# Seventy more products of the identity with itself, in front of two kinds of tile of a recurrence

## The chip, the cores and the metric

The kernel runs on 1 core of a Trainium2 chip. The metric is the device time of one execution in microseconds (us); the kernel before takes 1307.37 us, the median of 3 runs (1303.51 to 1311.31).

## The reference

The first stage is a recurrence. For each of 4 x 8 = 32 heads a state of 40 x 40 numbers is carried over 768 steps; inputs are r, k, v, w, a, b of shape (4, 8, 768, 40). Two products with weights follow on the 3072 x 320 result.

```
for t in range(768):
    y[t]  = r[t] @ state
    Sa    = state @ a[t]
    state = state * w[t][:, None] - outer(Sa, b[t]) + outer(v[t], k[t])
x = y, heads side by side                       # 3072 x 320
h = x @ moe_w_in;  x = (h * sigmoid(h)) @ moe_w_out      # 320 -> 2048 -> 320
out = (((x @ w1) * (x @ w2)) @ w3) @ w_out               # 320 -> 1024 -> 1024 -> 320
```

## The kernel before, in words

The recurrence is done in 12 chunks of 64 steps (`C`, `NCH`). Two heads share the 128 partitions, so there are 16 pairs, in 4 batches of 4. Inside a chunk the steps become small matrix products; only the state `Z` goes from chunk to chunk.

For two chunks at a time `prep` (L99) loads w, b, k, a and later r, clips w on DVE (L148), builds running products F and G on DVE (L106), multiplies the inputs by them, copies r into another layout on ACT (L207, `o<-in_`, from `in_r`), checks w with two ACTIVATE on ACT (L778, L779), and sends the results to DRAM; loads fetch them back in the layout of the products (`Rbd`, `Abd`, `Xt`, `Fn`). `A(c)` (L256) transposes (`px`, copied to `XT` by ACT at L267) and multiplies (`pl` L273). The 32 x 32 triangular blocks are inverted on POOL, and `merge` (L376) puts them together: TW is transposed on DVE (L380), `p` (L385, L397) are its products, ACT copies them (L387, L399).

`chain(c, b)` (L402) is the recurrence of one batch, in five steps with a `yield` between them; four chains are in flight. The steps are:

- `pp` (L414) and the old state `pss` (L423);
- `pu` (L435), copied into `UV` by DVE (L436) and ACT (L437). `UVb` is the `UV` of the fourth batch;
- `pz` (L443, L444), the products for the next state; DVE makes `Z` of it (L451, L452), and ACT copies `Z` into the next chunk's `UV` (L453, L454). Then `pv`, the transposes of `UV` (L457), copied to `VT` by ACT (L459). `VT` has two buffers;
- `pg` (L463), the products of `VT` with `Rbd`, masked into `GT` on DVE (L465);
- `py` (L472, L474), scaled into `x` on DVE (L477) and stored (`xd`) with SP.

`busy(p, n)` (L370; the rows call it L373) puts n products of the 128 x 128 identity with itself into a tile that the real products overwrite afterwards. It is called in front of `pu`, `pz` and the two `p` of `merge`. The numbers in front of it are: `MD` for `merge` (2 and 2 from chunk 2 on), `MC` = (0, 2) for `pu` and `pz`, and `MCC` = 2, the chunk from which `pu` and `pz` get none. So in the kernel before, chunks 0 and 1 have two such products before each `pz`, and no `pg` has any.

SP issues all DMAs, in order. Up to L1043 the order on the engines is that of the code; after it a list scheduler, run when the kernel is built, orders the instructions of every engine by its own estimate of when each can begin. An instruction that is added therefore moves others, on other engines too. From chunk 8 on, products for the weights (`w3ps` L581) and the first part of the second stage fill PE as well. After the recurrence `moe` (L658, L688) multiplies by the weights.

Of the kernel before, what the change touches and what calls it, by code (L numbers as in the profile page):

```python
# [24 lines left out]
class Kernel:  # L25
# [339 lines left out]
                s.nc.tensor.matmul(p, lhsT=s.idn, rhs=t[:, 0:512], start=True, stop=True)  # L365

    HC = 0
    MD, MC, MCC, ZT = (2, 2, 0), (0, 2), 2, 0

    def busy(s, p, n):  # L370

# [30 lines left out]
    def chain(s, c, b):  # L402
# [56 lines left out]
        ACT.copy(VT, pv[0:DP])  # L459
        yield 1280  # L460
        pg = s.PS([128, 4, 128], "pg")
        for hp in range(4):
            s.pe = nc.tensor.matmul(pg[:, hp], lhsT=VT[:, hp], rhs=Rbd[:, 4 * bb + hp], start=True, stop=True)  # L463
        GT = s.sm1.tile([128, 4, 128], F32, name="GT", bufs=2)
# [707 lines left out]
```

## Time and profile before

| | |
|---|---|
| median of 3 runs | 1307.37 us (1303.51 to 1311.31) |
| profiled execution | 1310.69 us, span 1309.0 us |
| PE busy | 1133.3 us (87%) |
| DVE, ACT, POOL busy | 695.7, 524.5, 309.8 us |
| granted TensorE clock, mean | 0.891 |

A row in time has its start, how long it ran, engine, line, operation, output and inputs, shapes and count; brackets hold the idle time of the engine just before and who ended it. PEclk is the granted clock of TensorE, as a share of 2.4 GHz: 0.50 is the lower of its two levels, 1.00 the upper. Lines are those of the kernel before; in the changed kernel lines after L368 stand one further down, lines after L461 two.

### The profile page before, as it was taken

How to read it: one execution, taken by the hardware profiler on the slowest of the kernel's cores; microseconds unless marked ns; L12 is line 12 of the kernel's file. 1: busy time of each engine (PE TensorE's matmuls, PEld its weight loads, DVE VectorE, ACT ScalarE, POOL GpSimd, SP SyncE). 2: the span in 40 equal slices, each digit the busy share in tenths (PEclk: the TensorE clock that was granted, in tenths of full speed). 3: DMA queues.
4: the chain of work that ended last, by engine and by line, in shares of the span. 5: the costliest groups of instructions: out<-in, count | busy, mean ns of one | idle time of the engine just before them, and what ended most of it. 6: DMA issues, size and time to landing. Idle time of an engine off the chain costs nothing. (4 is left out here: it accounts for less than half of the span.)

```text
span 1309.0 us, 25989 instructions
## 1 busy us (share of the span) xinstructions
PE 1133.3 (87%) x10416; PEld 995.9 (76%) x10416; DVE 695.7 (53%) x1358; ACT 524.5 (40%) x1156; POOL 309.8 (24%) x540
## 2 busy tenths in 40 slices
PE   2874768985978899997886999999999999999996
PEld 1654657885867888886675888889889889978985
DVE  7685772456487676758998531234424423433431
ACT  4555433353455454355455432233323323322321
POOL 4142600270551836503555102100000000000000
PEclk9885775687786899998988999999999999999998
DMA  9958787277388743667412000110001001000000
GB/s 211 192 101 180 135 145 145 48 137 159 69 175 196 146 106 75 192 175 217 121 31 61 1 1 1 36 27 20 1 1 41 1 1 36 6 1 21 1 1 23
DMA packets 258273, 105.86 MB, mean 81 GB/s; under 512 B 226400, under 2 KB 246880, under 8 KB 258144
## 3 DMA queue, kind: packets, MB, share of 16 engines
q1 hardware_dynamic: 258144, 104.12, 36.1%
q8 instruction: 84, 1.38, 0.5%
q14 instruction: 45, 0.37, 0.1%
HBM read 75.24 MB, written 28.84 MB: 80 GB/s over the span
## 5 line engine op out<-in xcount | busy, mean ns | idle before, releaser
L658 PE MATMUL hp<-xH,w 128*128 128x512 f32 x704 | 249.6, 397 | 2.7 <-ACT xH L487 2.7
L688 PE MATMUL yp<-w,gH 128*128 128x320 f32 x1152 | 234.0, 315 | 13.7 <-ACT gH L487 13.6
L666 DVE TENSOR_TENSOR sg<-sg,hp 128x512 f32<-128x512 f32 x144 | 99.0, 687 | 230.8 <-ACT sg L665 150.3
L688 PEld LDWEIGHTS yp<-w,gH 128*128 128x128 f32 x1152 | 193.1, 192 | 27.8 <-ACT gH L487 17.5
L487 ACT CAST gH<-sg 128x512 fp32r<-128x512 f32 x144 | 89.3, 620 | 161.7 <-DVE sg L666 106.1
L658 PEld LDWEIGHTS hp<-xH,w 128*128 128x128 f32 x704 | 131.8, 188 | 28.9 <-ACT xH L487 3.7
L488 DVE TENSOR_TENSOR gL<-sg,gH 128x512 fp32r<-128x512 f32 x120 | 83.0, 692 | 130.6 <-ACT gH L487 89.4
L688 PE MATMUL yp<-w,gL 128*128 128x320 f32 x576 | 147.5, 312 | 0.3 <-POOL gL L488 0.3
L658 PE MATMUL hp<-xL,w 128*128 128x512 f32 x352 | 139.2, 395 | 0.0
L688 PEld LDWEIGHTS yp<-w,gL 128*128 128x128 f32 x576 | 102.0, 190 | 2.4 <-POOL gL L488 0.7
L342 POOL TENSOR_TENSOR tmp<-T,L 128x87 f32<-128x87 f32 (+31 forms) x186 | 93.2, 501 | 42.3 <-DVE L L325 28.2
L665 ACT ACTIVATE sg<-hp 128x512 f32<-128x512 f32 x96 | 57.3, 597 | 109.3 <-PE hp L658 93.1
L346 POOL TENSOR_TENSOR T<-T,tmp 128x87 f32<-128x87 f32 (+31 forms) x186 | 96.8, 520 | 14.4
L273 PE MATMUL pl<-Abd,XT 104*128 104x128 f32 x384 | 66.4, 332 | 24.0 <-ACT XT L267 13.4
L273 PEld LDWEIGHTS pl<-Abd,XT 104*128 104x128 f32 x384 | 59.6, 238 | 26.9 <-ACT XT L267 12.8
L658 PEld LDWEIGHTS hp<-xL,w 128*128 128x128 f32 x352 | 66.4, 189 | 11.6
L463 PE MATMUL pg<-Rbd,VT 104*128 104x128 f32 x384 | 56.8, 309 | 21.2 <-ACT VT L459 15.5
L463 PEld LDWEIGHTS pg<-Rbd,VT 104*128 104x128 f32 x384 | 53.4, 220 | 23.0 <-ACT VT L459 16.8
L658 PE MATMUL hp<-xA,w 128*128 128x512 f32 x176 | 69.4, 395 | 0.0
L665 ACT COPY sg<-hp 128x512 f32<-128x512 f32 x48 | 28.2, 587 | 101.8 <-PE hp L658 64.5
L658 PE MATMUL hp<-xB,w 128*128 128x512 f32 x176 | 68.0, 394 | 0.0
L737 POOL COPY row<-row 128x64 f32<-128x64 f32 x24 | 5.5, 249 | 250.0 <-DVE row L700 142.8
(249 smaller groups left out, 2079.0 us busy)
## 6 DMA issues: line engine op xcount, KB each, us to landing
w3q<-in_moe_w_dram SPq DMA_DIRECT2D x16, 512.0 KB
wq<-in_moe_w_out_dram SPq DMA_DIRECT2D x24, 320.0 KB
wq<-in_moe_w_in_dram SPq DMA_DIRECT2D x16, 256.0 KB
wq<-in_moe_w_dram SPq DMA_DIRECT2D x16, 256.0 KB
Xt<-Bd SPq DMA_DIRECT2D x24, 160.0 KB
Xt<-Kd SPq DMA_DIRECT2D x24, 160.0 KB
Abd<-Ad SPq DMA_DIRECT2D x48, 80.0 KB
Fd<-F SPq DMA_DIRECT2D x12, 320.0 KB
```

Source lines behind the costliest of these rows:

```text
L273: nc.tensor.matmul(pl[:, hp], lhsT=XT[b][:, hp], rhs=Abd[b // 2][0:DP, 4 * (b % 2) + hp], start=True, stop=True)
L342: e.tensor_tensor(out=t3, in0=T[:, a:b, j : j + 1].to_broadcast([128, n, m]), in1=L[:, j : j + 1, j + 1 : 32].to_broadcast([128, n, m]), o ...
L346: s.last = e.tensor_tensor(out=T[:, a:b, j + 1 : 32], in0=T[:, a:b, j + 1 : 32], in1=t3, op=ALU.add)
L463: s.pe = nc.tensor.matmul(pg[:, hp], lhsT=VT[:, hp], rhs=Rbd[:, 4 * bb + hp], start=True, stop=True)
L487: s.nc.scalar.copy(hi, raw)
L488: (eng or s.nc.vector).tensor_tensor(out=lo, in0=raw, in1=hi, op=ALU.subtract)
L658: nc.tensor.matmul(p, lhsT=a, rhs=b, start=j == 0, stop=j == 7)
L665: nc.scalar.activation(out=sg, in_=p, func=func) if func else nc.scalar.copy(sg, p)
L666: nc.vector.tensor_tensor(out=sg, in0=sg, in1=q, op=ALU.mult)
L688: nc.tensor.matmul(y, lhsT=a[:, sl], rhs=W[:, b], start=first and j == 0, stop=last and j == 2)
L737: nc.gpsimd.tensor_copy(r[:, 320:384], r[:, 256:320])
```

## The change

`MCC` goes from 2 to 7, so the two products before `pz` are there for chunks 2 to 6 as well, in all four batches: 5 x 4 x 2 = 40. A new `MG` = (1, 6, 3) puts three products before `pg` in chunks 2 to 6 for batches 0 and 1: 5 x 2 x 3 = 30. Nothing that the kernel outputs depends on them.

```diff
-    MD, MC, MCC, ZT = (2, 2, 0), (0, 2), 2, 0
+    MD, MC, MCC, ZT = (2, 2, 0), (0, 2), 7, 0
+    MG = (1, 6, 3)
 ...
         pg = s.PS([128, 4, 128], "pg")
+        s.busy(pg, s.MG[2] if b < 2 and s.MG[0] < c <= s.MG[1] else 0)
         for hp in range(4):
```

The list scheduler also moves other instructions. The first place is ACT in chunk 5, from the second `VT` to the checks of `prep`; `UV` and `UVb` from `Z` are the next state's copies, `F` and `G` the first copies of `prep`. Before:

```order
L459 COPY VT<-pv 104x512
L150 COPY F<-in__3849 128x4x40
L151 COPY G<-in__3849 128x4x40
L453 COPY UV_595<-Z 40x4x40
L454 COPY UV_595<-Z 40x4x40
L453 COPY UV_595<-Z 40x4x40
L454 COPY UV_595<-Z 40x4x40
L459 COPY VT<-pv 104x512
L453 COPY UVb_597<-Z 40x4x40
L454 COPY UVb_597<-Z 40x4x40
L459 COPY VT<-pv 104x512
L778 ACTIVATE in__3849<-in__3849,small 128x1280
```

And in the changed kernel:

```order
L460 COPY VT<-pv 104x512
L454 COPY UV_595<-Z 40x4x40
L455 COPY UV_595<-Z 40x4x40
L454 COPY UV_595<-Z 40x4x40
L455 COPY UV_595<-Z 40x4x40
L454 COPY UVb_597<-Z 40x4x40
L455 COPY UVb_597<-Z 40x4x40
L780 ACTIVATE in__3891<-in__3891,small 128x1280
L460 COPY VT<-pv 104x512
L163 COPY G<-F 64x40
L781 ACTIVATE in__3891,small<-in__3891,small 128x1280
L460 COPY VT<-pv 104x512
```

The third `VT` stood behind six of the state's copies in chunk 5 and in front of the last two; now it stands behind all eight and behind the first check, and the fourth behind the second check.

The second place is ACT in chunk 6, around the copy of r (`o`), up to the first `UV` copy of the chunk. Before:

```order
L418 COPY Pb_233<-pp 64x4x40 x2
L429 COPY Sst_243<-pss 40x160 x2
L207 COPY o<-in__4495 128x1280
L267 COPY XT<-px 104x512
L418 COPY Pb_235<-pp 64x4x40 x2
L487 CAST wo_4693<-wr 128x320 x2
L429 COPY Sst_245<-pss 40x160 x2
L267 COPY XT<-px 104x512
L387 COPY TW<-p_4359 32x512 x2
L437 COPY UV_595<-pu 64x4x40
```

And in the changed kernel:

```order
L430 COPY Sst_243<-pss 40x160 x2
L267 COPY XT<-px 104x512
L489 CAST wo_4763<-wr 128x320 x2
L419 COPY Pb_235<-pp 64x4x40 x2
L430 COPY Sst_245<-pss 40x160 x2
L267 COPY XT<-px 104x512
L388 COPY TW<-p_4415 32x512 x2
L489 CAST wo_4874<-wr 128x320 x2
L207 COPY o<-in__4551 128x1280
L438 COPY UV_595<-pu 64x4x40
```

The copy of r stood in front of the third `XT`, and now stands behind `XT` and `TW`, just in front of the copy of the first `UV`.

The third place is SP at the end of chunk 5: the four loads of r for chunk 6 (`in_` from `in_r`), the stores of x (`xd`) and of the products (`Bd`, `Kd`, `Ad`), and the loads of `Fn`. Before:

```order
L51 DMA Fn<-Fd_81 64x8x40 x2
L51 DMA in__4495<-in_r_dram 32x1280
L51 DMA Fd_83<-F 64x1280 x2
L51 DMA in__4495<-in_r_dram 32x1280 x2
L51 DMA Rbd_227<-Rd_93 40x8x64 x2
L51 DMA w3q<-in_moe_w_dram 128x1024
L51 DMA in__4495<-in_r_dram 32x1280
L51 DMA wq_4240<-in_moe_w_out_dram 128x640
L51 DMA Bd_77<-in__3865 64x1280 x2
L51 DMA wq_4240<-in_moe_w_out_dram 128x640
L51 DMA Kd_71<-in__4128 64x1280 x2
L51 DMA xd_1_107<-x 256x1x40 x4
```

And in the changed kernel:

```order
L51 DMA Kd_71<-in__4184 64x1280 x2
L51 DMA Fn<-Fd_81 64x8x40 x2
L51 DMA Rbd_227<-Rd_93 40x8x64
L51 DMA xd_1_107<-x 256x1x40 x4
L51 DMA Rbd_227<-Rd_93 40x8x64
L51 DMA w3q<-in_moe_w_dram 128x1024 x2
L51 DMA Ad_89<-o 2560x1x32 x2
L51 DMA Fn<-Fd_81 64x8x40 x2
L51 DMA in__4551<-in_r_dram 32x1280 x4
L51 DMA wq_4296<-in_moe_w_out_dram 128x640 x2
```

The loads of r stood in front of the stores of `Bd`, `Kd` and the second `xd`; now they stand behind these, two `w3q`, `Ad` and two `Fn`.

## Rows read from the trace of the kernel before

**Rows 1.** Stretches of the span. Columns: the window and its length, busy time of each engine (instructions), PEclk, DMA share, GB/s.

```profile
180.00:640.00 460.00, 395.54 (x6044) 356.80 (x6044) 292.96 (x578) 216.84 (x543) 177.42 (x294) 0.82 0.62 140
193.50:241.00 47.50, 43.10 (x593) 38.76 (x593) 12.97 (x17) 16.75 (x38) 0.00 (x0) 0.50 0.62 119
251.50:265.00 13.50, 13.35 (x178) 12.69 (x180) 3.51 (x7) 3.03 (x10) 11.56 (x26) 0.50 0.22 46
337.00:343.50 6.50, 5.80 (x60) 4.69 (x60) 5.05 (x13) 5.36 (x15) 2.53 (x7) 0.50 0.23 50
374.50:381.00 6.50, 4.80 (x21) 4.71 (x22) 6.30 (x15) 2.46 (x6) 4.60 (x12) 0.50 1.10 199
388.00:398.00 10.00, 10.00 (x162) 9.18 (x161) 9.93 (x24) 4.30 (x13) 0.00 (x0) 0.50 0.60 142
421.00:425.50 4.50, 4.50 (x48) 3.43 (x48) 4.47 (x11) 3.47 (x11) 1.77 (x3) 0.51 0.89 137
```

**Rows 2.** PE in time, chunk 1. Start, duration, instruction, in brackets the idle time before it and its releaser.

```profile
184.40 0.61 PE L373 MATMUL pz<-idn 128*128 128x128 f32 x4
184.94 0.25 PE L443 MATMUL pz<-UV,Xt 128*64 128x40 f32 x1
...
193.30 4.03 PE L463 MATMUL pg<-Rbd,VT 104*128 104x128 f32 x16 [3.73 <-ACT VT L459]
```

**Rows 3.** PE in time: a product pg of chunks 2, 3, 5 and 6.

```profile
251.65 3.78 PE L463 MATMUL pg<-Rbd,VT 104*128 104x128 f32 x16 [2.16 <-ACT VT L459]
...
286.08 3.98 PE L463 MATMUL pg<-Rbd,VT 104*128 104x128 f32 x16 [3.95 <-ACT VT L459]
...
376.19 3.95 PE L463 MATMUL pg<-Rbd,VT 104*128 104x128 f32 x16 [4.40 <-ACT VT L459]
...
430.12 2.05 PE L463 MATMUL pg<-Rbd,VT 104*128 104x128 f32 x16 [0.60 <-ACT VT L459]
```

**Rows 4.** PE in time: before and in chunk 4, then before and in chunk 6.

```profile
308.91 1.92 PE L385 MATMUL p<-TW,L 32*32 32x32 f32 x64 [8.74 <-DVE TW L380]
...
340.18 0.29 PE L444 MATMUL pz<-UV,Xt 128*40 128x40 f32 x1 [0.70 <-ACT UV L437]
...
410.81 2.08 PE L273 MATMUL pl<-Abd,XT 104*128 104x128 f32 x8 [4.31 <-ACT XT L267]
...
421.21 0.33 PE L443 MATMUL pz<-UV,Xt 128*64 128x40 f32 x1
```

**Rows 5.** ACT in time, chunk 5: the third and fourth VT and a check.

```profile
375.56 0.58 ACT L459 COPY VT<-pv 104x512 f32<-104x512 f32 x1
377.43 0.58 ACT L459 COPY VT<-pv 104x512 f32<-104x512 f32 x1
382.30 1.36 ACT L778 ACTIVATE in__3849<-in__3849,small 128x1280 f32<-128x1280 f32 x1 [4.29 <-DVE G L106]
```

**Rows 6.** ACT and DVE in time: the r of chunk 6, and x of chunk 5.

```profile
407.48 2.67 ACT L207 COPY o<-in__4495 128x1280 f32<-128x1280 f32 x1 [6.96 <-DMA in__4495<-in_r_dram]
...
402.28 0.48 DVE L477 TENSOR_TENSOR x<-py,Fn 128x320 f32<-128x320 f32 x1
```

**Rows 7.** SP in time, chunks 5 to 6. Start, time at the queue's head, instruction.

```profile
394.13 1.29 SPq L51 DMA_DIRECT2D Fn<-Fd  x2
395.53 0.57 SPq L51 DMA_DIRECT2D in__4495<-in_r_dram  x1
...
401.73 0.82 SPq L51 DMA_DIRECT2D in__4495<-in_r_dram  x1
...
407.83 3.79 SPq L51 DMA_DIRECT2D xd<-x  x4
...
412.32 4.00 SPq L51 DMA_DIRECT2D Ad<-o  x2
416.37 3.20 SPq L51 DMA_DIRECT2D Fn<-Fd  x2
```

**Rows 8.** PE in time: a wait in chunk 8.

```profile
499.24 0.23 PE L444 MATMUL pz<-UV,Xt 128*40 128x40 f32 x1 [1.87 <-ACT UV L437]
```


## Prediction

> **What bounds the kernel now.** I first read the stretches of the span [rows 1]. Between 180 and 640 us, where the changed chunks lie, PE is busy for 395.5 of 460 us, but at a mean granted clock of 0.82: the clock goes between its two levels. It is at the lower one, 1.2 GHz, for example in 193.5-241, 251.5-265, 374.5-381 and 388-398. So PE is the bound there in two ways, by its work and by a clock that halves it, and the reader is to see that PE is busy in nearly the whole of some slow stretches (13.35 of 13.5 us).
>
> Then I read PE in time, with the idle time in front of each row. In chunks 2, 3 and 5 a `pg` waits for its `VT` copy, for 2.16, 3.95 and 4.40 us, and in chunk 6 for 0.60 [rows 3]; in each of the first three the clock is at the lower level right behind the wait. Other waits have nothing to do with `pg`: 8.74 us for `TW` at 308.91, which DVE makes late since the data of `prep` come late, and 4.31 us for `XT` at 410.81 [rows 4]. For that one I read ACT: `XT` stands behind the copy of r, which waits 6.96 us for its load [rows 6]. So in these chunks loads and the order on ACT and SP set the pace as often as PE's work.
>
> **The change, part by part.**
>
> *The products themselves.* Two products (a product leaves two records) begin at 184.40 and the next instruction at 184.94 [rows 2], at the upper clock: 0.27 us each, and I take twice that, 0.54, at the lower. Seventy cost 18.9 us of PE at the upper clock. In each of the chunks 2 to 6 it is 8 x 0.27 = 2.16 before `pz` and 6 x 0.27 = 1.62 before `pg`, 3.78 in all. What covers them are the waits that follow them on PE:
> - Chunks 3 and 5: waits of 3.95 and 4.40 [rows 3] hold the 3.78. Nothing is paid.
> - Chunk 2: 2.16 holds part, 1.6 is left over; but before chunk 4 PE has 8.74 us of idle time for `TW` [rows 4], set by loads. If that cover were gone, 1.6 us would be paid.
> - Chunk 4: its `pg` do not wait; a `pz` waits 0.70 [rows 4]. 3.78 - 0.70 = 3.1 are on PE's path. What comes next is chunk 6's first `pz`, which, below, is set by SP and ACT and not by PE, and so I count these 3.1 at nothing; the cover is the 4.31 us of idle time at 410.81. If it is gone they are paid in full.
> - Chunk 6: 3.78 - 0.60 = 3.2 at most [rows 3]. The first pair before `pz`, 0.54, lies in a wait (below), and the 1.62 before `pg` beside the wait for `VT`, whose copies ACT then does late. That leaves 2.16 - 0.54 = **+1.6**.
>
> *The third and fourth `VT` of chunk 5.* ACT did them at 375.56 and 377.43, and the first check at 382.30 [rows 5]. In the new order the third stands behind the last two state copies, which ended by 377.43, and behind the check of 1.36 us: 377.43 + 1.36 = 378.8, at least 3.2 us later. If the check runs no earlier than before, it is 382.30 + 1.36 = 383.7, 8.1 us later. The check waits for the products of `prep` on DVE, and the fewer masks stand among these, the earlier it can run; I take +3.6, near the lower end. Of this wait nothing is queued behind on PE but `pg`, `py` and the store of x; the price is paid through SP.
>
> *The copy of r of chunk 6.* This is the largest term. Before, its four loads left SP between 395.53 and 402.55, and the copy ran 4.9 us after that, at 407.48, for 2.67 us [rows 6, 7]. Now the loads stand behind the second `xd`, `Ad` and two `Fn`, and the first `UV` copy of chunk 6, which the first `pz` needs, stands behind the copy. SP is busy without a pause there, so taking the loads out lets it come earlier by what they then take again, and the last load leaves when the `Fn` did, at 416.37 + 3.20 = 419.57 [rows 7]. Then 4.9 to land, 2.67 to copy and about 0.3 for the `UV` copy give 427.5, against the first `pz` at 421.21 [rows 4]: +6.3. From below: the pair of `Fn` took only 1.29 at 394.13 [rows 7], so 1.9 of its 3.20 may be a wait that goes: +4.4. From above: the second `xd` needs x, written at 402.76 [rows 6]. With the third `VT` 3.6 later that is 406.4. Without the loads, which took at least 4 x 0.57 = 2.3, SP would come to it at 405.5; so SP waits 0.9: +7.2. With `VT` 5.7 later it would wait 3.0: +9.3. I take the middle of 4.4 and 7.2, **+5.8**. What goes in exchange, the wait of `XT` at 410.81, is worth nothing then, since `UV` is late next.
>
> *Chunk 8.* The scheduler moves twelve weight products into the 1.87 us in which a `pz` waits for `UV` [rows 8]. They have to be done anyway: **-1.9**.
>
> *The clock.* I take 0. A chunk that already has these products shows why: chunk 1 has two before each `pz`, and yet its `pg` waited 3.73 for `VT` at 193.30 and the clock was at 1.2 GHz from 193.5 to 241, though PE was busy for 43.1 of these 47.5 us [rows 1, 2]. The bounds are a gain of 14.8 (the first rival) and, where the clock falls in one more stretch like 388-398, a loss of half its 10.0 us, 5.0.
>
> The Trainium skill has a rule here, in "TensorE: Matmul & The Clock Gate", section "Part 4: PE-mode transpose": transposes do not count as activity for the clock in the way that products do. By it plain products put between transposes would be worth more than their busy time tells, which is the first rival. What the trace shows of it is mixed: the last 4.5 us before the clock rose at 425.5 held `pz` products and transposes in turn, with PE busy all the time [rows 1]; no row has transposes alone.
>
> The sum: 5.8 + 1.6 - 1.9 = +5.5. The profiled execution took 1310.7, so 1316.2 in its terms; it lies 3.3 above the median of the runs, which makes **1312.9**.
>
> **The rivals.**
>
> *A: the clock stays up (faster).* The added 3.78 us nearly fill the waits that the slow stretches follow. For it: in chunk 2 the wait of 2.16 is less than what is put in front of it, and in chunk 5 4.40 would be 0.6. If the clock rose in chunks 4 to 6, half of PE's busy time in the slow stretches would come back [rows 1]: 2.9 (337-343.5), 2.4 (374.5-381), 5.0 (388-398), 2.2 (421-425.5), 12.5 in all. With 3.1 + 3.2 paid for products and chunk 8's -1.9 this is -8.1, so 1299.3; with chunk 2's 13.35 / 2 = 6.7 carried through too, -14.8, 1292.6. I take the middle, **1296**. Against it: chunk 1, and that in chunk 5 the wait grows by what `VT` is later. Early gains must also pass 8.74 us of waiting for loads.
>
> *B: everything that I covered is paid (slower).* The place is SP. Chunk 4's 3.1 delay its x and with it the loads of `prep` queued behind; the third `VT` is 5.7 later, midway between its bounds; the copy of r then holds the first `pz` of chunk 6 by 9.3, and chunk 6 pays 3.2. 3.1 + 9.3 + 3.2 - 1.9 = +13.7, **1321**. It decides if the third `VT` of chunk 5 runs later than 380. For it: SP has hardly a pause in the rows, so what is late there stays late. Against: each of the three terms would have to come near its upper bound.
>
> *C: the products are hidden, and the order changes cancel.* Then it is 1307, inside the forecast's own range.
>
> **How the numbers follow.** The forecast, with C, has a chance of 0.45 and its own range is 1307 to 1317: below its middle if r's loads come early, above if the clock costs something. A has 0.27 (1292 to 1301), B 0.28 (1314 to 1325). This kernel can't be told from no change within 0.5%, 6.5 us: 1300.8 to 1313.9. Faster: 0.25 of A and 0.02 of the forecast, 0.27. Same: 0.33 of the forecast, 0.02 of A, 0.01 of B, 0.36. Slower: 0.10 of the forecast and 0.27 of B, 0.37. The range of 1295 to 1322 leaves out a third of A's chance and a third of B's, some 0.19.
>
> **What would show it.** Products at 0.27 and 0.54 us each. In chunks 2, 3 and 5: whether `pg`'s wait for `VT` shrinks by about 3.8, and whether the clock stays at 1.00 behind it; if it does in chunks 4 to 6, A is right. In chunk 5: the third `VT` against the last state copy. In chunk 6: the copy of r just in front of the first `UV` copy, its loads leaving SP behind `Fn`, and the first `pz` some 6 us later against the same chunk before; if the copy of r ends before PE is done with `pu`, my largest term is wrong and the result is near 1307 or below. In chunk 8: no wait of 1.87. From 640 on nothing should differ but a shift.

## The result and the profile after

The changed kernel took 1324.97 us (median of 4 runs, 1321.43 to 1326.06) against 1306.13 for the kernel before beside it (4 runs, 1303.51 to 1311.31): ratio 1.0141, 95% interval 1.0111 to 1.0170, or 18.8 us slower. The forecast of 1312.9 is wrong and so is its range, which ended at 1322. The profiled execution took 1324.17 us, 13.5 more than the one of before.

The products are there. Lines of the source in the changed kernel, between 180 and 450 us: operation, count, then the shortest, the median and the longest record in ns. A product leaves two records, and 8 of the 88 belong to chunk 1.

```profile
L374 PE MATMUL pz<-idn x88: 273/275/421, 180.5 to 431.5; 128*128 128x128 f32 x88
L374 PE MATMUL pg<-idn x60: 273/275/275, 239.7 to 435.4; 128*128 128x128 f32 x60
```

The clock did rise. To compare the same work in kernels that run at different times, I use the second addition `x` (`x<-py`, DVE) of a chunk as a mark. From chunk 1's mark to the last `x`, the kernel before and then the changed kernel; the third row is a stretch of the changed kernel in chunk 6:

```profile
211.28:628.56 417.28, 359.43 (x5620) 324.06 (x5617) 260.76 (x516) 200.47 (x506) 170.16 (x288) 0.83 0.62 139
206.80:639.31 432.51, 363.24 (x5760) 330.01 (x5757) 259.85 (x517) 200.43 (x506) 178.72 (x288) 0.87 0.60 134
416.00:432.00 16.00, 8.89 (x74) 7.74 (x75) 13.08 (x26) 11.15 (x22) 5.11 (x9) 0.50 0.80 156
```

The mean granted clock is 0.87 where it was 0.83. PE has 140 records more, the 70 products, and its busy time grew by 3.8 us only, from 359.4 to 363.2, though the products alone are 18.9 at the upper clock. The stretch grew by 15.2. So three quarters of what grew, 11.4 us, is time in which PE waits. The third row is one place, chunk 6, where PE is busy for 8.9 of 16 us.

PE in time, changed kernel: a `pg` of chunk 3, a `pg` and a `p` of chunk 5, and a `pz` of chunk 6.

```profile
280.28 4.28 PE L465 MATMUL pg<-Rbd,VT 104*128 104x128 f32 x16 [7.17 <-ACT VT L460]
...
372.24 4.27 PE L465 MATMUL pg<-Rbd,VT 104*128 104x128 f32 x16 [4.79 <-ACT VT L460]
...
383.62 1.92 PE L386 MATMUL p<-TW,L 32*32 32x32 f32 x64 [3.45 <-DVE TW L381]
...
419.67 0.29 PE L445 MATMUL pz<-UV,Xt 128*40 128x40 f32 x1 [7.50 <-ACT UV L438]
```

The wait of `pg` in chunk 5 did not shrink from 4.40 by the products [rows 3], it is 4.79. Chunk 3's grew from 3.95 to 7.17. The 7.50 before `pz` in chunk 6 answers to no wait at all [rows 4]. ACT in the same kernel, chunk 5 and then chunk 6:

```profile
370.35 1.36 ACT L780 ACTIVATE in__3891<-in__3891,small 128x1280 f32<-128x1280 f32 x1
371.62 0.56 ACT L460 COPY VT<-pv 104x512 f32<-104x512 f32 x1
...
416.63 2.67 ACT L207 COPY o<-in__4551 128x1280 f32<-128x1280 f32 x1 [9.42 <-DMA in__4551<-in_r_dram]
419.33 0.29 ACT L438 COPY UV<-pu 64x160 f32<-64x160 f32 x1
```

The check of 1.36 us stands right in front of the third `VT`, and the copy of r, 2.67 us, right in front of the first `UV`. Both are as the order said. The time of r's loads on SP, at the queue's head:

```profile
389.35 3.91 SPq L51 DMA_DIRECT2D xd<-x  x4
...
407.38 3.54 SPq L51 DMA_DIRECT2D Fn<-Fd  x2
410.97 2.99 SPq L51 DMA_DIRECT2D in__4551<-in_r_dram  x4
```

The last load of r leaves at 413.96 and the copy starts 2.7 us later; before, SP's last left at 402.55 and the copy ran at 407.48 [rows 6, 7].

To place the loss in time I go by the marks, in one execution each. *Chunks 2 to 4* runs from chunk 1's mark to chunk 4's, *5 and 6* from there to chunk 6's, *7 on* to the last `x`, *behind* to the end of the span. The kernels below the second row are the experiments.

| us in the profiled execution | chunks 2 to 4 | 5 and 6 | 7 on | behind |
|---|---|---|---|---|
| before | 144.2 | 80.9 | 192.1 | 680.4 |
| after | 140.9 | 95.0 | 196.6 | 683.1 |
| products_old_order | 142.7 | 82.7 | 195.2 | 680.9 |
| new_order_no_products | 146.9 | 92.6 | 193.2 | 681.7 |
| new_order_in_chunk_5 | 140.2 | 89.6 | 195.0 | 681.3 |
| new_order_in_chunk_6 | 138.7 | 88.0 | 193.7 | 681.5 |
| new_order_in_5_6 | 138.1 | 95.2 | 192.9 | 680.9 |
| new_order_to_chunk_4 | 147.2 | 82.3 | 194.3 | 681.5 |
| new_order_but_5_6 | 146.8 | 84.3 | 196.6 | 681.1 |
| loads_early | 141.8 | 86.4 | 195.1 | 683.2 |

Chunks 5 and 6 took 14.1 us longer than before. The 3.3 gained ahead of them are within what executions differ by: the kernels with before's order and the products took from 138.1 to 142.7 there. The new order gains nothing in chunks 2 to 4 and may lose there. In eight traces with the products and the new order up to chunk 4 (further kernels below among them), chunk 4's mark comes at 347.7 to 355.5 us, 351.8 in the mean; in the seven with the products and before's order there, at 343.5 to 352.3, 347.8 in the mean.

### The profile page after: what moved, and what is told of

Read it like the earlier page. It is cut to its first block, busy times and chain, and to the rows that moved or that the text cites. A ratio compares the mean times of both kernels' runs of the same rounds, so it can differ in the third digit from the quotient of the medians.

```text
span 1322.4 us, 26273 instructions
## 1 busy us (share of the span) xinstructions
PE 1135.7 (86%) x10556; PEld 999.1 (76%) x10556; DVE 695.9 (53%) x1358; ACT 524.8 (40%) x1156; POOL 318.5 (24%) x540
## 5 line engine op out<-in xcount | busy, mean ns | idle before, releaser
L690 PE MATMUL yp<-w,gH 128*128 128x320 f32 x1152 | 232.2, 314 | 12.4 <-ACT gH L489 12.3
L342 POOL TENSOR_TENSOR tmp<-T,L 128x87 f32<-128x87 f32 (+31 forms) x186 | 98.5, 530 | 40.5 <-DVE L L325 26.2
L346 POOL TENSOR_TENSOR T<-T,tmp 128x87 f32<-128x87 f32 (+31 forms) x186 | 100.4, 540 | 14.3
L273 PE MATMUL pl<-Abd,XT 104*128 104x128 f32 x384 | 59.3, 307 | 23.0 <-ACT XT L267 12.0
L465 PE MATMUL pg<-Rbd,VT 104*128 104x128 f32 x384 | 55.8, 301 | 24.8 <-ACT VT L460 18.8
L273 PEld LDWEIGHTS pl<-Abd,XT 104*128 104x128 f32 x384 | 53.4, 216 | 25.3 <-ACT XT L267 13.1
```

The costliest lines, as they stand in the source:

```text
L273: nc.tensor.matmul(pl[:, hp], lhsT=XT[b][:, hp], rhs=Abd[b // 2][0:DP, 4 * (b % 2) + hp], start=True, stop=True)
L342: e.tensor_tensor(out=t3, in0=T[:, a:b, j : j + 1].to_broadcast([128, n, m]), in1=L[:, j : j + 1, j + 1 : 32].to_broadcast([128, n, m]), o ...
L346: s.last = e.tensor_tensor(out=T[:, a:b, j + 1 : 32], in0=T[:, a:b, j + 1 : 32], in1=t3, op=ALU.add)
L690: nc.tensor.matmul(y, lhsT=a[:, sl], rhs=W[:, b], start=first and j == 0, stop=last and j == 2)
```

## The experiments

All times are ratios to runs of before on the same chip, with 95% intervals; us are these times 1307.

**Products or order?** A table lists each engine's instructions in a wanted order, and each is made to follow the one before it by an order-only dependency (`NoSync`):

```diff
+    def fix(s, packed, extra):
...
+                        s.tc.add_manual_dep(k, last.name, info, reason="fix")
...
+            s.fix(ORDER, s.added)
```

No run holds the kernel before to its own order and changes nothing else, so what this itself may cost is in the figures that follow.

*products_old_order* has the 70 products and before's order:

> All 70 products of the change, but every instruction on every engine in the order of the kernel before, by order-only dependencies; a product stands just in front of the pz or pg that it belongs to. Theory O (the moved order is the loss, above all the copy of r in front of the first UV copy of chunk 6; the products with the clock are a gain): 1295 to 1302, with the waits of pg in chunks 2, 3 and 5 shorter and more of 180 to 420 us at the upper clock. Rival P (the products' own time on PE is the loss): 70 x 0.27 = 18.9 more than before, about 1325. Rival C (products hidden and clock gains lost to loads): 1306, within 3.

Measured: 1.0037 (1.0010 to 1.0065), median 1310.71. *new_order_no_products* has the changed kernel's order and none of the products:

> None of the 70 products, but every instruction on every engine in the order of the changed kernel. Theory O: slower than the changed kernel or equal, 1322 to 1335, with the copy of r of chunk 6 again just in front of the first UV copy and PE waiting about 7 us there. Rival P: 1306, as before. Rival C: 1325, as the changed kernel.

Measured: 1.0143 (1.0094 to 1.0192), median 1326.58, the whole loss without the work that was added. In before's order the products cost some 4.8 us (1.3 to 8.5) of their 18.9; the order costs the rest, some 13.6. In the new order they cost nothing more that these runs can tell. The clock shows what the products give back. From chunk 1's mark to chunk 4's, before and then products_old_order:

```profile
211.28:355.53 144.25, 117.96 (x1717) 105.84 (x1714) 67.40 (x129) 63.09 (x148) 47.47 (x91) 0.71 0.57 105
```

```profile
205.90:348.55 142.65, 121.79 (x1801) 110.95 (x1797) 68.16 (x128) 63.27 (x148) 49.80 (x92) 0.78 0.55 106
```

The granted clock there is 0.78 with the products and 0.71 without. In new_order_no_products it is 0.74 and in the changed kernel 0.83. Over all kernels here it is 0.71 to 0.76 in the three that lack the products in these chunks, and 0.76 to 0.83 in the others.

*chunks_2_to_4* keeps the products in chunks 2 to 4 alone and lets the scheduler order anew:

```diff
-    MD, MC, MCC, ZT = (2, 2, 0), (0, 2), 7, 0
-    MG = (1, 6, 3)
+    MD, MC, MCC, ZT = (2, 2, 0), (0, 2), 5, 0
+    MG = (1, 4, 3)
```

> The products only in chunks 2 to 4 (24 before pz, 18 before pg), the order left to the scheduler, which puts the copy of r of chunk 6 behind most of that chunk's UV copies. Theory O: the early gain of the changed kernel (7 us at chunk 5) without the loss of chunk 6: 1296 to 1303. Rival P: 42 x 0.27 = 11.3 more than before, 1317.

Measured: 1.0090 (1.0063 to 1.0118). Slower too, in a third order. Its profiled execution was the shortest of ten, 1309.06 against a median of 1318.92, and so doesn't say where.

**Is it the copy of r in chunk 6?** *r_after_uv* holds that copy behind the `UV` copies:

```diff
-        ACT.copy(o, r.rearrange("p t e -> p e t"))
+        with s.tc.issue_after(s.uv.ins) if g == 5 else ExitStack():
+            ACT.copy(o, r.rearrange("p t e -> p e t"))
```

The scheduler then moves some other instructions too, further on in the program.

> The changed kernel, with the copy of r of chunk 6 put behind the copies of UV of that chunk on ACT (one order-only dependency; the scheduler then moves a few other instructions). Its load leaves SP as late as in the changed kernel. Theory O: the wait of 7.50 us of the first pz of chunk 6 goes and the time falls by 8 to 14, to 1311 to 1317. Rival P and a rival in which that wait only hides another one: within 3 of 1325.

Measured: 1.0142 (1.0088 to 1.0196), nothing won. PE still waits in front of `pz`, for DVE's copy `A` now (DVE's row below):

```profile
421.50 1.22 PE L375 MATMUL pz<-idn 128*128 128x128 f32 x4 [7.65 <-DVE A L275]
```

```profile
419.99 0.33 DVE L499 TENSOR_SCALAR wr<-wq 128x320 int32<-128x320 int32 x1 [11.42 <-DMA wq<-in_moe_w_out_dram]
```

In the new order a weight tile `wr` that waits 11.42 us for its load stands in front of the copies that PE needs. The next three take it, and then the loads:

*weights_moved* (DVE, chunk 6; its cast `wo` on ACT goes along):

```diff
 TENSOR_TENSOR A<-pl,msk
-TENSOR_SCALAR wr<-wq
-SCALAR_TENSOR_TENSOR wr<-wq,wr
-TENSOR_TENSOR A<-pl,msk
-TENSOR_SCALAR wr<-wq
...
+TENSOR_SCALAR wr<-wq
+SCALAR_TENSOR_TENSOR wr<-wq,wr
 TENSOR_TENSOR Z<-pz,Z
```

> As the run before, but only the weight tile's conversion is moved; the copy of r stays in front of the first UV copy of chunk 6. Theory D: the copy of r still holds the first pz, 1321 to 1327. Rival E (the weight tile alone was the cause, and the copy of r is beside it): 1312 to 1317.

*r_and_weights_moved* has both edits:

> The changed kernel with its products, every instruction in the order of the changed kernel by order-only dependencies, but two things moved behind the last UV copy (UVb) of chunk 6: the copy of r on ACT, and on DVE the conversion of one weight tile (six wr<-wq, with the first of the two casts on ACT and the subtraction on POOL that follow it). Theory D (two waits lie side by side in chunk 6: ACT waits for the load of r, DVE for the load of a weight tile that SP issues just behind it, and either alone holds the first pz): the wait of 7.5 us goes, chunk 6 is reached 8 to 11 us earlier, 1312 to 1317. Rival S (the loss is spread over many moved instructions): within 4 of 1325.

*loads_early* has neither, and puts the four loads of r on SP behind the first `Fn`, in front of the second `xd`, and two loads of the weight tile in front of `Ad`:

```diff
 DMA Fn<-Fd
+DMA in_<-in_r_dram x4
 DMA Rbd<-Rd
...
+DMA wq<-in_moe_w_out_dram x2
 DMA Ad<-o
 DMA Fn<-Fd
-DMA in_<-in_r_dram x4
-DMA wq<-in_moe_w_out_dram x2
```

> The changed kernel with its products and its order, but on SP alone the four loads of r of chunk 6 stand in front of the second xd of chunk 5 (behind the first two Fn), and the two loads of the weight tile in front of Ad. ACT and DVE keep their order. Theory D: both waits shrink by most of their 7 to 10 us and the time falls by 6 to 10, 1315 to 1319, since the place on ACT and DVE only costs because SP brings the data late. Rival S: within 4 of 1325.

Measured: 1.0138 (1.0104 to 1.0171), 1.0123 (1.0099 to 1.0148) and 1.0119 (1.0088 to 1.0150). None brings back more than 3 us in the median. With both moved the wait before `pz` did go, and two others came, for a `VT` that now stands behind the copy of r. PE, r_and_weights_moved:

```profile
417.83 0.23 PE L450 MATMUL pz<-UV,Xt 128*40 128x40 f32 x1 [0.82 <-ACT UV L443]
...
426.75 0.94 PE L377 MATMUL pg<-idn 128*128 128x128 f32 x6 [3.01 <-ACT VT L465]
...
432.59 3.79 PE L470 MATMUL pg<-Rbd,VT 104*128 104x128 f32 x16 [4.01 <-ACT VT L465]
```

**Which chunk's order?** All with the 70 products; each takes the new order in a part of the program and before's elsewhere, so products_old_order (1.0037) is what to hold them against:

> All 70 products. Every engine in the order of the changed kernel up to the moment at which the second x of chunk 4 began in its trace, from there in the order of the kernel before. Theory L (the order costs its time in chunk 6, where the copy of r and a weight tile wait for late loads): 1307 to 1314, as the run with the products in the old order (1310.7). Rival F (five): the same. Rival S (spread, or early): 1316 or more.

> All 70 products; the order of the changed kernel only for what ran between the second x of chunk 4 and the second x of chunk 5 (third and fourth VT behind the checks, GT, TD and TW behind the products of prep), else the order of before. Theory L: 1309 to 1315. Rival F (the late VT, GT and TW of chunk 5 are the loss, and the waits of chunk 6 lie beside what they delay): 1318 to 1325.

> All 70 products; the order of the changed kernel only for what ran between the second x of chunk 5 and the second x of chunk 6, else the order of before. That holds the copy of r in front of UV, its late loads on SP, and the weight tile on DVE. Theory L: 1318 to 1325, with PE waiting 5 us or more at the first pz of chunk 6. Rival F: 1309 to 1314.

> All 70 products; the order of before up to the second x of chunk 6, from there that of the changed kernel. Theory L: 1309 to 1314 (the marks of x in the trace show 1 to 2 us between chunk 6 and the end). Rival S: 1316 or more.

> All 70 products; the order of the changed kernel only between the second x of chunk 4 and the second x of chunk 6. If chunks 5 and 6 hold the loss: 1320 to 1326, as the changed kernel. If the loss is spread: 1313 to 1318.

> All 70 products; the order of the changed kernel everywhere but between the second x of chunk 4 and the second x of chunk 6, where it is that of before. If chunks 5 and 6 hold the loss: 1309 to 1314, as the products in the old order (1310.7) with the 0.8 and 0.9 us that the order before and behind cost by themselves. If the loss is spread: 1316 to 1322.

| new order in | ratio (95%) | over 1.0037, us |
|---|---|---|
| chunks to 4 | 1.0043 (1.0007 to 1.0079) | 0.8 |
| chunk 5 | 1.0119 (1.0063 to 1.0175) | 10.7 |
| chunk 6 | 1.0075 (1.0045 to 1.0106) | 5.0 |
| from chunk 7 | 1.0044 (1.0012 to 1.0076) | 0.9 |
| 5 and 6 | 1.0118 (1.0095 to 1.0140) | 10.6 |
| all but 5 and 6 | 1.0086 (1.0062 to 1.0110) | 6.4 |

Chunks 5 and 6 hold most of the order's price, chunk 5 the larger part. The parts don't add up: 10.6 and 6.4 are more than the 13.6 of the whole, and to chunk 4 and from 7 alone cost next to nothing, though without 5 and 6 they cost 6.4. The intervals, from 6 to 15 us wide, allow for much of that. The table of marks is sharper for 5 and 6: kernels with before's order there took 82.3 to 84.3 us, and with the new order in both 92.6 to 95.2 (loads_early apart). These rows are that stretch in products_old_order, with chunk 5's order, with chunk 6's, and in the changed kernel:

```profile
348.55:431.24 82.69, 74.26 (x1190) 67.92 (x1190) 59.32 (x119) 42.65 (x102) 37.11 (x63) 0.81 0.83 174
```

```profile
349.19:438.74 89.55, 76.47 (x1190) 69.82 (x1190) 58.22 (x118) 42.44 (x102) 37.41 (x63) 0.79 0.80 162
```

```profile
345.89:433.85 87.96, 73.05 (x1190) 66.49 (x1190) 57.29 (x119) 42.40 (x102) 37.61 (x66) 0.83 0.77 165
```

```profile
347.74:442.73 94.99, 74.73 (x1190) 68.33 (x1190) 58.58 (x119) 42.48 (x102) 38.94 (x65) 0.78 0.73 153
```

The same 1190 instructions on PE each time. Chunk 5's order adds 6.9 us and chunk 6's 5.3, together 12.1; the changed kernel has 12.3 more. PE's idle time is 8.4, 13.1, 14.9 and 20.3 us. The sums agree, but it isn't the same waits added. The last load of r leaves SP 47.4 us after chunk 4's mark in products_old_order, 52.7 with chunk 5's order, 46.2 with chunk 6's, and 66.2 in the changed kernel, which has both. So with chunk 6's order alone the copy of r waits for no load, and PE doesn't wait behind it; PE waits behind a weight tile on DVE. ACT, DVE and PE in new_order_in_chunk_6:

```profile
403.61 2.68 ACT L210 COPY o<-in__4551 128x1280 f32<-128x1280 f32 x1
...
410.93 0.33 DVE L503 TENSOR_SCALAR wr<-wq 128x320 int32<-128x320 int32 x1 [7.26 <-DMA wq<-in_moe_w_out_dram]
...
417.51 0.43 PE L449 MATMUL pz<-UV,Xt 128*64 128x40 f32 x2 [3.84 <-DVE UV L442]
```

**How chunk 5's order costs chunk 6 its time.** PE in products_old_order, chunk 5, and the first wait of chunk 6:

```profile
369.71 1.16 PE L470 MATMUL pg<-Rbd,VT 104*128 104x128 f32 x8 [1.44 <-ACT VT L465]
...
376.77 0.29 PE L481 MATMUL py<-Sst,Rbd 104*64 104x40 f32 x4
378.30 1.92 PE L391 MATMUL p<-TW,L 32*32 32x32 f32 x64 [1.23 <-DVE TW L386]
...
404.62 2.08 PE L276 MATMUL pl<-Abd,XT 104*128 104x128 f32 x8 [4.69 <-ACT XT L270]
```

And in new_order_in_chunk_5:

```profile
374.62 4.27 PE L470 MATMUL pg<-Rbd,VT 104*128 104x128 f32 x16 [5.71 <-ACT VT L465]
...
382.30 0.29 PE L481 MATMUL py<-Sst,Rbd 104*64 104x40 f32 x4
385.21 1.92 PE L391 MATMUL p<-TW,L 32*32 32x32 f32 x64 [2.62 <-DVE TW L386]
...
410.85 1.72 PE L276 MATMUL pl<-Abd,XT 104*128 104x128 f32 x8 [2.85 <-ACT XT L270]
```

Waits of 9.3 us in chunk 5 where there were 3.2: 3.7 more for `VT`, 2.4 more for `TW`, which DVE and ACT do later too (two more waits for `VT` and `TW`, 0.53 in the first kernel and 0.97 in the second, are in these sums). The first `x` of chunk 5 comes 6.3 us later after chunk 4's mark (390.25 - 349.19 = 41.1, against 383.29 - 348.55 = 34.7). The waits for `VT` and `TW` are not the reason. The first `x` needs the `py` of the first two batches, and the `VT` that PE waits for are those of the other two. Its `py` was done at 377.06 and at 382.59, and `x` began 6.2 and 7.7 us after that. What it stands behind is DVE's own queue. Stretches from chunk 4's mark to the first `x` of chunk 5 (the third busy time is DVE's), products_old_order and then new_order_in_chunk_5:

```profile
348.55:383.29 34.74, 31.47 (x498) 28.86 (x499) 25.62 (x54) 17.99 (x45) 21.03 (x37) 0.88 0.82 164
```

```profile
349.19:390.25 41.06, 31.64 (x513) 28.75 (x514) 29.61 (x66) 18.13 (x46) 21.85 (x36) 0.84 0.80 158
```

DVE does 12 instructions and 4.0 us more ahead of `x`, and is idle for 2.3 us more. The new order puts multiplications of `prep` and a weight tile there. DVE in new_order_in_chunk_5; no idle time stands in front of `x`:

```profile
379.15 1.28 DVE L109 TENSOR_TENSOR F<-F 128x1120 f32<-128x1120 f32 x1
380.35 1.32 DVE L109 TENSOR_TENSOR G<-G 128x1120 f32<-128x1120 f32 x1
...
388.25 1.48 DVE L109 TENSOR_TENSOR in__3907<-in__3907,G 128x1280 f32<-128x1280 f32 x1
...
390.25 0.48 DVE L484 TENSOR_TENSOR x<-py,Fn 128x320 f32<-128x320 f32 x1
```

SP, products_old_order and then new_order_in_chunk_5:

```profile
383.80 2.52 SPq L54 DMA_DIRECT2D xd<-x  x4
...
388.71 0.57 SPq L54 DMA_DIRECT2D in__4551<-in_r_dram  x1
...
394.85 1.08 SPq L54 DMA_DIRECT2D in__4551<-in_r_dram  x1
```

```profile
390.94 3.80 SPq L54 DMA_DIRECT2D xd<-x  x4
...
398.55 1.55 SPq L54 DMA_DIRECT2D in__4551<-in_r_dram  x3
...
401.44 0.42 SPq L54 DMA_DIRECT2D in__4551<-in_r_dram  x1
```

The store of the first `x` stands in front of r's loads in both, and the last of them leaves 5.9 us later (5.3 from chunk 4's mark). The copy of r, ACT, in the one and the other:

```profile
401.29 2.67 ACT L210 COPY o<-in__4551 128x1280 f32<-128x1280 f32 x1 [7.34 <-DMA in__4551<-in_r_dram]
```

```profile
407.51 2.67 ACT L210 COPY o<-in__4551 128x1280 f32<-128x1280 f32 x1 [5.53 <-DMA in__4551<-in_r_dram]
```

6.2 later (5.6 from the mark), and so is `pl` behind `XT` (410.85 against 404.62). That is the chain as these two traces show it: more work on DVE ahead of the first `x`, late store of `x`, late loads of r, late copy of r, late chunk 6. Of the 6.9 us, 1.7 are there by the second `x` of chunk 5 (48.2 against 46.5 after the mark) and 5.2 come in chunk 6. No run takes the work of `prep` from in front of `x`, so the head of the chain is read and not tested. loads_early agrees in its trace, where chunks 5 and 6 took 86.4 us in place of 95.0; but that was the shortest of its four executions (1315.93; the others 1321.56 to 1327.71), so it shows what is possible there and not what is usual.

**Which part of chunk 5?** From new_order_in_chunk_5, *chunk_5_vt_back* changes ACT alone and *chunk_5_tw_back* DVE alone:

```diff
+COPY VT<-pv
 COPY UVb<-Z
+COPY VT<-pv
 ACTIVATE in_<-in_,small
-COPY VT<-pv
...
-COPY VT<-pv
```

```diff
 TENSOR_TENSOR GT<-pg,msk
+STREAM_TRANSPOSE TD<-T
+COPY Lc<-A
+STREAM_TRANSPOSE TW<-TD
 TENSOR_TENSOR FCn<-F,G
```

*four_places_undone* takes the changed kernel's order with both of these, r_and_weights_moved and loads_early.

> As the run with the new order in chunk 5 alone (1317.6), but on ACT the third and fourth VT of chunk 5 stand again in front of the last state copies and of the two checks. Theory V (the late VT is the loss of chunk 5): the wait of 5.71 us of pg shrinks to about 2, the time to 1310 to 1314. Rival W (TD and TW stand behind the products of prep on DVE, and the merge is late with or without VT): 1315 to 1319.

> As the run with the new order in chunk 5 alone (1317.6), but on DVE the transpose TD, the four Lc copies and the first TW stand right behind the second GT of the chunk, in front of the rest of prep's products and a weight conversion; VT stays late. Theory V: pg still waits 5 to 6 us, 1314 to 1319. Rival W: TW some 5 us earlier, 1310 to 1314.

> The changed kernel with its products and its order, and four places undone: VT of chunk 5 in front of the checks, TD and TW right behind GT, the copy of r and the weight tile of chunk 6 behind its UV copies, and their loads earlier on SP. If these places are the loss: 1309 to 1315. If it is spread further: 1317 to 1324.

Measured: 1.0057 (1.0036 to 1.0078), 1.0076 (1.0050 to 1.0102) and 1.0089 (1.0058 to 1.0119). By the ratios `VT` gives back some 8 us and `TW` some 6, of 10.7; each interval meets that of new_order_in_chunk_5, and the two traces don't show it. Chunks 5 and 6 took 90.0 and 91.4 us in them, against 89.6: one wait went and the other was as long or longer. The first `x` stayed late too, 41.7 and 40.1 us after chunk 4's mark against 41.1, since the work of `prep` still stands in front of it on DVE, and the copy of r ran 59.0 and 59.4 us after the mark against 58.3. PE, chunk_5_vt_back, its first `x` on DVE, and then PE in chunk_5_tw_back:

```profile
374.49 1.16 PE L470 MATMUL pg<-Rbd,VT 104*128 104x128 f32 x8 [2.49 <-ACT VT L465]
...
381.58 0.29 PE L481 MATMUL py<-Sst,Rbd 104*64 104x40 f32 x4
388.92 1.92 PE L391 MATMUL p<-TW,L 32*32 32x32 f32 x64 [7.05 <-DVE TW L386]
...
393.96 0.48 DVE L484 TENSOR_TENSOR x<-py,Fn 128x320 f32<-128x320 f32 x1
```

```profile
369.39 4.28 PE L470 MATMUL pg<-Rbd,VT 104*128 104x128 f32 x16 [6.04 <-ACT VT L465]
```

With `VT` back, the `py` of the first two batches was done 12.1 us before `x`, so the late `VT` isn't what `x` waits for. These are the longest of 12 executions (1320.65) and the shortest of 6 (1310.29), and I take no price from them. All four places together bring 6.8 of the 18.4 us. In the trace, the longest of six executions, the first `x` of chunk 5 is still 39.1 us behind the mark, and the copy of r, moved away from `UV`, holds up a `VT` of chunk 6. PE, four_places_undone:

```profile
432.68 3.78 PE L470 MATMUL pg<-Rbd,VT 104*128 104x128 f32 x16 [5.86 <-ACT VT L465]
```

**A faster kernel.** *old_order_r_later* has no products and before's order, with the copies of r of chunks 4 and 6 behind the `UV` copies of their chunk, and their stores `Rd` later on SP:

```diff
-COPY o<-in_
 COPY XT<-px
...
 COPY UVb<-pu
+COPY o<-in_
```

> The kernel before, without the 70 products, in its own order, but with the copies of r of chunks 4 and 6 behind the last UV copy of their chunk on ACT, and their stores behind the next Abd loads on SP. In the profile of before PE waits 4.05 and 4.31 us at these places, for XT or TW that stand behind the copy of r. If those waits set the pace, 1299 to 1303; if the loads behind them on SP are late next (another wait in their place), 1304 to 1308.

*products_r_later* is the same with the products:

> All 70 products in the order of before, with the copies of r of chunks 4 and 6 behind the last UV copies of their chunks, as in the run without products that took 1303.6. If the products are hidden by the waits for r (4.05 and 4.31 us in the kernel before), they cost more here than the 3.9 us that they cost with those waits in place: 1309 to 1315. If they are hidden elsewhere or pay for themselves by the clock: 1301 to 1307.

Measured: 0.9954 (0.9930 to 0.9979), median 1303.56, and 0.9981 (0.9959 to 1.0004). The first beats both kernels, by 6.0 us (2.7 to 9.1) against before. In its one trace the gain stands in chunks 2 to 4 (137.1 us) and from 7 on (189.3), not in 5 and 6 (86.7), so which of the two copies brings it I can't say. The products cost some 3.5 there as well by the ratios; the intervals of the two meet, so this isn't clear of nothing.

## Why the prediction was wrong

**The failing step** is the price of chunk 5's new order: "Of this wait nothing is queued behind on PE but `pg`, `py` and the store of x; the price is paid through SP". I priced one moved instruction, the late `VT`, through the second `xd` alone, where it was worth 0.9, and gave DVE's part of the new order no term. How late the copy is I had right: from chunk 4's mark the third `VT` came 3.9 us later than before, and I took 3.6. But `x` doesn't move with it. The second `x` came 1.3 later, and the first, which needs neither the third nor the fourth `VT`, 6.3 later in new_order_in_chunk_5, behind 4.0 us more work on DVE. Its store stands on SP ahead of r's loads in before already (391.01, in front of the first load at 395.53 [rows 7]). So chunk 5's order is worth 6.9 us by the traces and 10.7 (some 8 either way) by the ratios; in my sum it was worth less than 1.

**The copy of r in chunk 6, +5.8.** The first `pz` came 6.3 us later than before, counted from chunk 4's mark (419.67 - 347.74 against 421.21 - 355.53), it waits 7.50, and the copy stands in front of `UV` as said. In part that is luck: the last load left 66.2 us after the mark where I had 64.0, and the copy began 2.7 us after it where I had 4.9. As a cause the copy is too narrow. Taking it away from there brings nothing (r_after_uv), since the weight tile on DVE is as late. Chunk 6's order alone costs 5.3 by the traces and 5.0 by the ratios, near my term, but there the copy of r holds nothing up (new_order_in_chunk_6), so that agreement is luck.

**Chunk 6 behind the first `pz`, +1.6**, is the other term that was far off. From the first `pz` to the second `x` of chunk 6, before and then the changed kernel:

```profile
421.21:436.46 15.25, 14.65 (x258) 13.15 (x257) 11.69 (x27) 8.57 (x23) 11.80 (x21) 0.86 0.94 148
419.67:442.73 23.06, 19.62 (x279) 18.23 (x279) 15.48 (x31) 10.63 (x26) 14.51 (x27) 0.72 0.51 85
```

That is 7.8 more: PE is busy for 5.0 more, at a lower granted clock, and idle for 2.8 more. Without the products it is 18.5 us (new_order_no_products, 432.26 to 450.77), so the order alone adds 3.3 there.

**The products.** 0.27 us each as said. For the cost on PE's path I had 1.6 of 18.9; measured in before's order it is 4.8 (1.3 to 8.5). The waits that were to cover them did so in part: in products_old_order `pg` waits 2.0 of 4.40 us in chunk 5 and not at all in chunk 2, but 4.6 in chunk 3, where it was 3.95. The new order put a longer wait there, 7.17.

**Chunk 8, -1.9**: the wait did go; no `pz` of chunk 8 waits now, but one of chunk 9 waits 1.82 for `UV`, which none did before. From 7 on the changed kernel is 4.5 us longer in its trace, and that part of the order alone costs 0.9 (-3.3 to 5.1 by its own interval). Nothing was won.

**The clock, 0**: it rose, as rival A has it, and I had given too little to that. It rose in chunks 2 to 4 (0.71 to 0.83), not in 5 and 6 (0.79 and 0.78), and A needed it in chunks 4 to 6. The rule of the Trainium skill ("TensorE: Matmul & The Clock Gate", section "Part 4: PE-mode transpose") fits the rise; no run tells products that fill a wait from products that count where transposes don't.

**Rival B**, 1321, came nearest in time, 4 us short. Its condition, a third `VT` later than 380, was not met (371.62, with chunk 4's mark 7.8 earlier than before), so it was near by luck. **Rival C** falls by its number; products_old_order at 1.0037 is what it would have looked like.

**What stays open**: the 6.4 us of the order outside chunks 5 and 6, whose two halves cost 0.8 and 0.9 alone. By the marks the place is likely ahead of chunk 5: with the new order chunk 4's mark comes 4.0 us later in the mean of eight traces than in the mean of seven with before's order. Single executions overlap, and no run says which wait in there it is.

## What to carry to other kernels

When a list scheduler sets the order, an instruction that is added costs what it moves: run the new order without the new work, and the new work in the old order, before arguing about either. Price every engine's new order, not only the instruction that you saw move: find the first store with loads behind it on the in-order queue, and see what its producer stands behind. If that producer has no idle time in front of it, its own engine's order sets it, and an earlier input brings nothing. Undoing one place of an order can bring nothing, because the next late thing was waiting beside it.

## What the hardware showed unexpectedly

70 products with 18.9 us of PE time cost 4.8 us (1.3 to 8.5) in before's order, while the granted clock in chunks 2 to 4 went from 0.71 to 0.78. And kernels of one order differ between executions by 10 us and more (chunk_5_vt_back: 1307.61 to 1320.65 in 12), so one trace can show where a wait is, and seldom what it costs.
